# Low halves of a split made by GpSimd instead of VectorE, in the weight conversion and batch 0 of a pack-attention and softplus feed-forward kernel

## Chip, cores and metric

One core of one Trainium2 chip runs the whole program. The time is microseconds on the device for one execution. A core has five engines that run side by side, each through its own instructions in order: TensorE (PE in the profile, its weight loads PEld), VectorE (DVE), ScalarE (ACT), GpSimd (POOL) and SyncE (SP), which here issues nearly all transfers.

## What is computed

For each of 8 batches, 8 heads, 576 rows of 64: 32 packed queries attend to all rows, the rows then attend to the 32 packed results, and the heads are joined to x of 4608 x 512. A feed-forward layer follows.

```python
p_packed = sm_attn(p, k, v)
out = sm_attn(q, p_packed, p_packed)
x = out.transpose(0, 2, 1, 3).reshape(B * S, H * D)
h = x @ w_in                                        # 512 x 2048
g = np.maximum(h, 0.0) + np.log1p(np.exp(-np.abs(h)))   # softplus
return (g @ w_out).astype(np.float32)               # 2048 x 512
```

w_in and w_out come as 64-bit floats; the kernel converts them to 32 bits itself.

## The kernel before

**Units.** The feed-forward part is a loop over 128 units: batch b (8) by slice f of 128 hidden columns (16). A unit has a first product (gemm1, L600), softplus (L622 to L631), and a second product (gemm2_tile, L638), which runs two units later (LAG = 2) and adds to four accumulators acc. The packed results are folded into w_in (make_m, L563), for two slices at a time in batch 0, so that a unit's first product multiplies attention weights with m.

**Split products.** TensorE multiplies in a reduced 32-bit format (F32R), so each factor is split in a high part, the value cast to that format, and a low part, the value less the high part, and a product is three: high by high, high by low, low by high. The halves are at_h and at_l (attention weights, L545 and L546), mh and ml (L578, L579), wo_h and wo_l (w_out, L238 and L244), gh and gl (softplus' result, L614 and L615).

**Softplus of a unit.** ScalarE takes the absolute value of both halves of the product ph (L622), then exp and log (L624, L625; in batch 0 over 576 columns at once). VectorE adds max(h, 0) (L627), which also sets ph free for the next unit, as there are two buffers. Of the 576 rows, GpSimd copies the last 64 into rest (L631). `split` makes gh and gl of the other 512. e has two buffers, gh and gl three each.

**Weight conversion.** `convert` goes through 32 blocks n, 16 of w_in and 16 of w_out. For each, SyncE loads the 64-bit block; ScalarE makes m (L200) and r (L204) from its words; VectorE makes t (a bit mask, L206, and a shift with an or, L211); GpSimd adds t and r as integers (L219), into w_in_sb for a block of w_in and into r for one of w_out. For w_out ScalarE then casts t to wo_h (L238), and wo_l is r less wo_h. m has one buffer and r two for most blocks, so a block's r can be overwritten only when wo_l of an earlier block has been made. Conversion begins before batch 0's attention and goes on through batch 0, beside batch 1's attention.

**What sets the order.** TensorE runs in the order of the code. On the other engines a scheduler orders the instructions from priorities and its own estimate of durations, so a change of engine moves others too. Each engine runs its queue strictly in order.

Of the kernel before, what the change touches and what calls it, by code (L numbers as in the profile page):

```python
# [9 lines left out]
F32 = mybir.dt.float32  # L10
F32R = mybir.dt.float32r
AF = mybir.ActivationFunctionType
ALU = mybir.AluOpType
# [13 lines left out]
def pack_attention_then_softplus_ffn(  # L27
# [10 lines left out]
    nc = tc.nc  # L38
# [3 lines left out]
    P = 128  # L42
# [7 lines left out]
    NT = S // P  # L50
# [26 lines left out]
    def rest_at(b, f):  # L77

        return f + NF if f < LAG and b // 2 % 2 else f
# [69 lines left out]
    def load64(srcs, nm, place):  # L149
        if place is None:  # L150
            x = cv.tile([P, CN], I64, tag="x", name=f"x_{nm}", bufs=2)
        else:
            x = rest[:, place:place + 8, :].rearrange("x f j -> x (f j)").bitcast(I64)
        n = P // len(srcs)
        for i, src in enumerate(srcs):
            nc.sync.dma_start(
                x[i * n:(i + 1) * n].rearrange("x (a n) -> x a n", a=src.shape[1]), src
            )
        return x
# [13 lines left out]
    def convert(order):  # L173

        srcs = {"i": w_in_src, "o": w_out_src}

        places, until = [None, None, LAG, LAG + 8], [len(order), len(order), 6, 16]  # L180
        xs, ts, rs, at = {}, {}, {}, {}

        def prefetch(place):
            n = len(at)
            if n < len(order):
                w, i = order[n]
                at[n] = place
                xs[n] = load64(srcs[w](i), f"{w}{i}", places[place])

        def first(n):  # L190
            x = xs.pop(n)
            lo = x.bitcast(U32).rearrange("x (n two) -> x n two", two=2)[:, :, 0]
            hi = x.bitcast(I32).rearrange("x (n two) -> x n two", two=2)[:, :, 1]
            pool, tm, tr, tt = (work, "gh", "gl", "gh") if spare and n % 2 else (cv, "m", "r", "t")

            m = pool.tile([P, CN], F32, tag=tm, name=f"m_{n}", bufs=LAG + 1 if pool is work else 1)
            nc.scalar.activation(m, hi.bitcast(F32), AF.Copy, scale=2.0**-112)  # L200


            r = pool.tile([P, CN], I32, tag=tr, name=f"r_{n}", bufs=LAG + 1 if pool is work else 2)
            nc.scalar.activation(r, lo, AF.Copy, scale=2.0**-29)  # L204
            t = pool.tile([P, CN], I32, tag=tt, name=f"t_{n}", bufs=LAG + 1 if pool is work else 2)
            nc.vector.tensor_scalar(t, m.bitcast(I32), -0x80000000, None, op0=ALU.bitwise_and)  # L206
            ts[n], rs[n] = (t, m), r

        def second(n):
            t, m = ts[n]  # L210
            nc.vector.scalar_tensor_tensor(  # L211
                t, m.bitcast(I32), 3, t, op0=ALU.logical_shift_left, op1=ALU.bitwise_or
            )
            w, i = order[n]
            dst, a = rs[n], 1
            if w == "i":
                dst, a = w_in_sb.bitcast(I32)[:, :, i * P:(i + 1) * P], DM // P
            v = [y.rearrange("x (a n) -> x a n", a=a) for y in (t, rs[n])]
            nc.gpsimd.tensor_tensor(  # L219
                dst if a > 1 else dst.rearrange("x (a n) -> x a n", a=a), *v, op=ALU.add  # L220
            )

        for n in range(2):
            prefetch(n)
        yield
        for n in range(2, 4):
            prefetch(n)
        yield
        for n in range(len(order) + 1):
            if n < len(order):  # L230
                first(n)
                if n < until[at[n]]:
                    prefetch(at[n])
            yield
            w, i = order[n - 1] if n else ("i", 0)
            t = ts.pop(n - 1)[0].bitcast(F32) if n else None
            if w == "o":
                nc.scalar.copy(wo_h[:, i, :], t)  # L238
            yield
            if n < len(order):  # L240
                second(n)
            yield
            if w == "o":
                nc.vector.tensor_tensor(  # L244
                    wo_l[:, i, :], rs[n - 1].bitcast(F32), wo_h[:, i, :].bitcast(F32),
                    op=ALU.subtract,
                )
                yield
# [358 lines left out]
    def halves(nm):  # L607
        return [
            work.tile([P, NT * P], F32R, tag=t, name=f"{t}_{nm}", bufs=LAG + 1)
            for t in ("gh", "gl")  # L610
        ]

    def split(hi, lo, x):
        nc.vector.tensor_copy(hi, x)  # L614
        nc.vector.tensor_tensor(lo, x, hi.bitcast(F32), op=ALU.subtract)  # L615

    def softplus(b, f, hv, done):
        e = work.tile([P, S], F32, tag="e", name=f"e_{b}_{f}")
        es = [e[:, c * C:(c + 1) * C] for c in range(2)]
        spans = [e] if b == 0 else es  # L620
        for c in range(2):
            nc.scalar.activation(es[c], hv[c], AF.Abs)  # L622
            for x in spans[c:c + 1] if b else spans[:c]:
                nc.scalar.activation(x, x, AF.Exp, scale=-1.0)  # L624
                nc.scalar.activation(x, x, AF.Ln, bias=1.0)  # L625
        for c in range(2):
            nc.vector.scalar_tensor_tensor(es[c], hv[c], 0.0, es[c], op0=ALU.max, op1=ALU.add)  # L627
        yield
        yield
        r = (b % 2) * REST  # L630
        nc.gpsimd.tensor_copy(rest[:, rest_at(b, f), r:r + REST], e[:, NT * P:])  # L631
        yield
        done[b, f] = halves(f"{b}_{f}")
        split(*done[b, f], e[:, :NT * P])

    def gemm2_tile(acc, gh, gl, f, cs, first, last):
        for i, (x, y) in enumerate(((gh, wo_h), (gh, wo_l), (gl, wo_h))):
# [28 lines left out]
    def rests(b):  # L666


        fs = sorted(range(NF), key=lambda x: rest_at(b, x))
        gh, gl = halves(f"{b}_m")  # L670
        n = NT // 2
        for i in range(0, NF, n):
            o = rest_at(b, fs[i])
            c = i % NT * P
            cs = slice(c, c + n * P)
            split(gh[:, cs], gl[:, cs], rest[:, o:o + n, :].rearrange("x f j -> x (f j)"))
            if i == 0:
                yield
                am = ps_acc.tile([P, DM], F32, tag="acc", name=f"acc_{b}_m")
            for t in range(n):  # L680
                gemm2_tile(
                    am, gh, gl, fs[i + t], slice(c + t * P, c + (t + 1) * P),
                    i + t == 0, i + t == NF - 1,
                )
        store(am, [(0, b - 1, NT * P, REST), (REST, b, NT * P, REST)], f"{b}_m", NT)
        yield
# [14 lines left out]

    pt = load_pack(0, (nc.sync, nc.scalar))
    conv = convert(order)
    for g in range(G):
        load("k", 0, g)
# [31 lines left out]
    for u in range(len(units) + LAG):  # L737
        if u < len(units):
            b, f = units[u]
            if f == 0:  # L740
                if (b + 1) % BG == 0 and b + 1 < B:
                    pack_transposed((b + 1) // BG, pt)
                ahead = attention(b + 1) if b + 1 < B else iter(())
                due = 0.0
            chain = softplus(b, f, gemm1(b, f, res[b]), gs)
            next(chain)
            if f == NF - 1:
                if (b + 2) % BG == 0 and b + 2 < B:
                    pt = load_pack((b + 2) // BG, (nc.sync,))
                for _ in ahead:  # L750
                    pass
                if b + 1 < B:
                    weights(b + 1)
# [64 lines left out]
```

## Time and profile before

| | before |
|---|---|
| median of 3 runs | 772.86 us (772.16 to 773.06) |
| the profiled execution | 772.16 us, span 770.4 us |
| TensorE busy | 730.1 us (95%), mean clock 0.98 |
| VectorE, ScalarE, GpSimd busy | 530.7, 433.4, 98.7 us |
| L244 (wo_l) on VectorE | 16, mean 899 ns, all in the first 160 us |
| L615 (gl) on VectorE | 128 over the span, mean 684 ns |
| L219 on GpSimd | 32 in the first 160 us, 44.9 us |

A row of the timeline gives start, length (us), engine, line, operation, output<-inputs with partitions x elements, and in brackets how long the engine had been idle and what released it. A row of the windows gives a stretch, its length, and busy time and count of each engine (of one line, when asked for one), then the granted TensorE clock, the share of the transfer engines and GB/s. The time of an instruction includes what it waits inside the engine once it has begun, so that one kind can show several lengths. A row of the waits gives who waited, for whom, total, times and longest. The chain of waits goes back from the last instruction by what released each.

### The profile page before, as it was taken

To read this page: it belongs to the slowest core of one execution; us is meant where nothing else is said; L and a number is where in the kernel's file an instruction comes from. 1 tells how busy PE (TensorE), PEld (TensorE's weight loads), DVE (VectorE), ACT (ScalarE), POOL (GpSimd) and SP (SyncE) were. 2 spreads that over 40 slices of the span, in tenths; PEclk is the share of its full clock that TensorE was granted. 3 is DMA by queue.
4 is the path that set the end of the run, shared out by engine and by line. 5 is a ranking of instruction groups with operands and counts; after the bars stand their busy time and mean duration, and the time that the engine had idled before them with its cause. 6 is when DMAs were issued, how large, how long until landed. Compare 5 with 4: busy or idle time off the path is not lost.

```text
span 770.4 us, 14175 instructions
## 1 busy us (share of the span) xinstructions
PE 730.1 (95%) x5360; PEld 579.0 (75%) x5360; DVE 530.7 (69%) x1092; ACT 433.4 (56%) x1057; POOL 98.7 (13%) x166
## 2 busy tenths in 40 slices
PE   6557998999999999999999999999999999999997
PEld 4335776787787877887788877877887877888886
DVE  2696879975787568675877568675877558665554
ACT  5667977665555455565455355565555364555540
POOL 1143444200000000000000000000000000000110
PEclk9957999999999999999999999999999999999999
DMA  9877755534312144033312134033312210010002
GB/s 210 231 192 171 180 149 134 123 73 74 65 31 71 30 64 92 1 94 62 68 26 70 31 63 93 1 86 62 63 32 60 40 31 1 1 55 1 1 1 69
DMA packets 149668, 55.97 MB, mean 73 GB/s; under 512 B 116320, under 2 KB 142944, under 8 KB 149600
## 3 DMA queue, kind: packets, MB, share of 16 engines
q1 hardware_dynamic: 149328, 55.00, 32.1%
q8 instruction: 42, 0.69, 0.4%
q14 instruction: 26, 0.21, 0.1%
q10 hardware_dynamic: 272, 0.07, 0.0%
HBM read 45.61 MB, written 9.44 MB: 71 GB/s over the span
## 4 chain that ended last, share of the span: by engine, by line
PE 83%; DVE 6%; ACT 5%; DMA 4%; issue 1%; POOL 1%; SPq 0%; ACTq 0%; DVEq 0%; POOLq 0%
PE acc L638 41%; PE ph L600 26%; PE acc_m L638 6%; PE psm L563 4%; PE ps L277 3%; DMA rest<-in_moe_w_out 2%; DVE at_l L546 1%; PE ps L320 1%; PE psa L312 1%; DMA x_i<-in_moe_w_in 1%; ACT e L624 1%; DVE e L627 1%; ACT m L200 1%; ACT e L622 1%; DVE t L206 1%
## 5 line engine op out<-in xcount | busy, mean ns | idle before, releaser
L638 PE MATMUL acc<-wo_h,gh 128*128 128x512 f32 x512 | 207.7, 406 | 0.0
L627 DVE SCALAR_TENSOR_TENSOR e<-ph,e 128x288 f32<-128x288 f32 x256 | 114.1, 454 | 133.4 <-ACT e L625 130.7
L622 ACT ACTIVATE e<-ph 128x288 f32<-128x288 f32 x256 | 103.0, 403 | 179.5 <-PE ph L600 155.0
L638 PE MATMUL acc<-wo_l,gh 128*128 128x512 f32 x512 | 201.4, 393 | 0.0
L638 PE MATMUL acc<-wo_h,gl 128*128 128x512 f32 x512 | 201.1, 393 | 0.0
L600 PE MATMUL ph<-at_h,mh 128*128 128x288 f32 x512 | 158.5, 309 | 13.1 <-ACT at_h L545 7.2
L600 PE MATMUL ph<-at_l,mh 128*128 128x288 f32 x512 | 153.4, 300 | 3.7 <-DVE at_l L546 3.7
L600 PE MATMUL ph<-at_h,ml 128*128 128x288 f32 x512 | 152.8, 299 | 0.0
L600 PEld LDWEIGHTS ph<-at_h,mh 128*128 128x128 f32 x512 | 97.7, 191 | 48.0 <-DVE gl L615 15.1
L631 POOL COPY rest<-e 128x64 f32<-128x64 f32 x128 | 53.3, 417 | 575.7 <-DVE e L627 542.9
L638 PEld LDWEIGHTS acc<-wo_h,gh 128*128 128x128 f32 x512 | 96.4, 188 | 26.9 <-issue 12.3
L638 PEld LDWEIGHTS acc<-wo_h,gl 128*128 128x128 f32 x512 | 96.3, 188 | 21.2
L624 ACT ACTIVATE e<-e 128x288 f32<-128x288 f32 (+1 forms) x240 | 109.4, 456 | 3.9
L625 ACT ACTIVATE e<-e 128x288 f32<-128x288 f32 (+1 forms) x240 | 109.3, 456 | 3.0
L638 PEld LDWEIGHTS acc<-wo_l,gh 128*128 128x128 f32 x512 | 96.6, 189 | 13.1
L600 PEld LDWEIGHTS ph<-at_l,mh 128*128 128x128 f32 x512 | 97.9, 191 | 8.4 <-DVE at_l L546 5.3
L600 PEld LDWEIGHTS ph<-at_h,ml 128*128 128x128 f32 x512 | 97.9, 191 | 0.0
L615 DVE TENSOR_TENSOR gl<-e,gh 128x512 fp32r<-128x512 f32 x128 | 87.6, 684 | 6.3
L578 ACT CAST mh<-psm 128x512 fp32r<-128x512 f32 (+1 forms) x72 | 36.3, 540 | 60.8 <-PE psm L563 60.6
L614 DVE CAST gh<-e 128x512 fp32r<-128x512 f32 x128 | 55.5, 434 | 5.9
L579 DVE TENSOR_TENSOR ml<-psm,mh 128x512 fp32r<-128x512 f32 (+1 forms) x72 | 43.0, 624 | 22.0 <-ACT mh L578 21.8
L563 PE MATMUL psm<-w_in_sb,pt 64*32 64x512 f32 (+1 forms) x576 | 40.9, 560 | 8.2 <-ACT T_k L269 4.8
(84 smaller groups left out, 694.8 us busy)
## 6 DMA issues: line engine op xcount, KB each, us to landing
v<-in_v SPq DMA_DIRECT2D x16, 576.0 KB, 5.4
x_i<-in_moe_w_in SPq DMA_DIRECT2D x28, 256.0 KB, 4.5
k<-in_k SPq DMA_DIRECT2D x48, 144.0 KB, 3.3
q<-in_q SPq DMA_DIRECT2D x48, 144.0 KB, 3.4
x_o<-in_moe_w_out SPq DMA_DIRECT2D x11, 512.0 KB, 3.7
out<-o SPq DMA_DIRECT2D x18, 256.0 KB, 2.5
rest<-in_moe_w_out SPq DMA_DIRECT2D x5, 512.0 KB, 6.2
k<-in_k SPq DMA_DIRECT2D x4, 576.0 KB, 6.1
```

Source lines behind the costliest of these rows:

```text
L563: nc.tensor.matmul(ps[hh * J:(hh + 1) * J, :n], res["pt"][g][o:o + D, hh * J:(hh + 1) * J], w_in_sb[o:o + D, hh, c * n:(c + 1) * n], start ...
L578: nc.scalar.copy(mh[:, cols], ps[:, :n])
L579: nc.vector.tensor_tensor(ml[:, cols], ps[:, :n], mh[:, cols].bitcast(F32), op=ALU.subtract)
L600: nc.tensor.matmul(ph[:, :C], x[:, ms], y[:, g, cs], start=(i == 0), stop=(i == 3 * G - 1),)
L614: nc.vector.tensor_copy(hi, x)
L615: nc.vector.tensor_tensor(lo, x, hi.bitcast(F32), op=ALU.subtract)
L622: nc.scalar.activation(es[c], hv[c], AF.Abs)
L624: nc.scalar.activation(x, x, AF.Exp, scale=-1.0)
L625: nc.scalar.activation(x, x, AF.Ln, bias=1.0)
L627: nc.vector.scalar_tensor_tensor(es[c], hv[c], 0.0, es[c], op0=ALU.max, op1=ALU.add)
L631: nc.gpsimd.tensor_copy(rest[:, rest_at(b, f), r:r + REST], e[:, NT * P:])
L638: nc.tensor.matmul(acc, x[:, cs], y[:, f, :], start=(first and i == 0), stop=(last and i == 2),)
```

## The change

wo_l of all 16 w_out blocks and gl of batch 0's 16 units go from VectorE to GpSimd. The other batches' gl stays on VectorE, and so does every gh.

```diff
             if w == "o":
-                nc.vector.tensor_tensor(
+                nc.gpsimd.tensor_tensor(
                     wo_l[:, i, :], rs[n - 1].bitcast(F32), wo_h[:, i, :].bitcast(F32),
                     op=ALU.subtract,
                 )
...
-    def split(hi, lo, x):
+    def split(hi, lo, x, engine=None):
         nc.vector.tensor_copy(hi, x)
-        nc.vector.tensor_tensor(lo, x, hi.bitcast(F32), op=ALU.subtract)
+        (engine or nc.vector).tensor_tensor(lo, x, hi.bitcast(F32), op=ALU.subtract)
...
-        split(*done[b, f], e[:, :NT * P])
+        split(*done[b, f], e[:, :NT * P], None if b else nc.gpsimd)
```

TensorE's order is the same in both. VectorE has 32 instructions less, GpSimd 32 more. In the rows below a number behind a name tells tiles of one name apart; e_0 and gl_0 are of unit 0; t_334, r_332 and t_363, r_361 belong to the w_out blocks of slices 2 and 3, t_460, r_458, m_456 and t_561, r_559, m_557 to the next two w_in blocks, and r_581, m_579 to the w_out block behind these.

ScalarE, at the first unit of batch 0, before:

```order
L622 ACTIVATE e_0_541<-ph_0_1_534 128x288 [waits PE_49]
L624 ACTIVATE e_0_541<-e_0_541 128x576 [waits Activation_49]
L238 CAST wo_h<-t_334 128x512 [waits DVE_49]
L200 ACTIVATE m_456<-x_i_246 128x512
L238 CAST wo_h<-t_363 128x512 [waits DVE_49]
L625 ACTIVATE e_0_541<-e_0_541 128x576 [waits Activation_49]
L269 COPY T_k_0_0_555<-psT_k_0_0_551 128x288 [waits PE_49]
```

And with the change:

```order
L238 CAST wo_h<-t_363 128x512 [waits DVE_49]
L622 ACTIVATE e_0_541<-ph_0_1_534 128x288 [waits PE_49]
L204 ACTIVATE r_559<-x_i_288 128x512 [waits DMAHW7_49,DMAHW6_49,Pool_49]
L624 ACTIVATE e_0_541<-e_0_541 128x576 [waits Activation_49]
L200 ACTIVATE m_557<-x_i_288 128x512 [waits DVE_49]
L625 ACTIVATE e_0_541<-e_0_541 128x576 [waits Activation_49]
L204 ACTIVATE r_581<-rest 128x512 [waits DMAHW0_49,Pool_49]
L200 ACTIVATE m_579<-rest 128x512 [waits DVE_49,Activation_49]
L269 COPY T_k_0_0_555<-psT_k_0_0_551 128x288 [waits PE_49]
```

The conversions of two blocks moved ahead of unit 0's exp and log, and r_559, which waits for GpSimd, stands ahead of both.

GpSimd, at the same place, with the change:

```order
L219 TENSOR_TENSOR r_332<-t_334,r_332 128x512 [waits DVE_49,Activation_49]
L219 TENSOR_TENSOR r_361<-t_363,r_361 128x512 [waits DVE_49,Activation_49]
L244 TENSOR_TENSOR wo_l<-r_332,wo_h 128x512 [waits Activation_49,Pool_49]
L244 TENSOR_TENSOR wo_l<-r_361,wo_h 128x512 [waits Activation_49,Pool_49]
L219 TENSOR_TENSOR w_in_sb<-t_460,r_458 128x4x128 [waits DVE_49]
L219 TENSOR_TENSOR w_in_sb<-t_561,r_559 128x4x128 [waits DVE_49,Activation_49]
L631 COPY rest<-e_0_541 128x64 [waits DVE_49,Activation_49]
L615 TENSOR_TENSOR gl_0_570<-e_0_541,gh_0_569 128x512 [waits DVE_49]
```

The two wo_l stand behind both adds and ahead of the two w_in blocks; before, the queue had only the adds and the copy.

GpSimd, in the middle of batch 0 (units 8 and 9), as the difference:

```order
 L219 TENSOR_TENSOR r_1163<-t_1165,r_1163 128x512
+L244 TENSOR_TENSOR wo_l<-r_1163,wo_h 128x512
 L219 TENSOR_TENSOR r_1189<-t_1191,r_1189 128x512
+L244 TENSOR_TENSOR wo_l<-r_1189,wo_h 128x512
 L631 COPY rest<-e_8_1211 128x64
+L615 TENSOR_TENSOR gl_8_1277<-e_8_1211,gh_8_1276 128x512
 L219 TENSOR_TENSOR w_in_sb<-t_1265,r_1263 128x4x128
 L631 COPY rest<-e_9_1320 128x64
+L615 TENSOR_TENSOR gl_9_1363<-e_9_1320,gh_9_1362 128x512
```

Four subtracts of 128x512 join three adds and two small copies there.

## The prediction

> **What bounds the kernel now.** I read the page first: its busy shares and the slices, for the stretch in which TensorE is not full.
>
> ```profile
> PE 730.1 (95%) x5360; PEld 579.0 (75%) x5360; DVE 530.7 (69%) x1092; ACT 433.4 (56%) x1057; POOL 98.7 (13%) x166
> PE   6557998999999999999999999999999999999997
> DVE  2696879975787568675877568675877558665554
> POOL 1143444200000000000000000000000000000110
> PEclk9957999999999999999999999999999999999999
> ```
>
> A slice is 19 us. TensorE is short of full only in the first eight, and just there VectorE and GpSimd are busiest: this is where the weights are converted and batch 0 runs. Behind it TensorE is the bound and the change does nothing. Next I read the windows of the stretch and who made TensorE wait from 60 to 165 us.
>
> ```profile
> 45.00:70.00 25.00, 17.45 (x107) 12.63 (x105) 19.39 (x33) 16.39 (x34) 11.08 (x10) 0.57 0.71 177
> 70.00:136.00 66.00, 60.32 (x513) 45.00 (x511) 56.61 (x119) 55.30 (x117) 30.56 (x28) 1.00 0.63 165
> 136.00:158.00 22.00, 21.74 (x148) 17.41 (x133) 20.44 (x40) 15.29 (x32) 4.80 (x6) 1.00 0.46 89
> PE ph L600 <- DVE e L627: 5.9, 5, 2.8
> PE psm L563 <- POOL w_in_sb L219: 1.7, 1, 1.7
> ```
>
> The columns are window, length, then PE, PEld, DVE, ACT, POOL busy, clock, DMA. From 70 to 136 us TensorE is busy 60.3 of 66 us, VectorE 56.6, ScalarE 55.3, GpSimd 30.6. TensorE's waits after 60 us add up to about 7.6 us, and end in VectorE's softplus row and GpSimd's weight row. By busy shares alone GpSimd has room and VectorE has none, so the shift looks good. What the shares do not tell is whether the two can work at the same time. The timeline of both tells it:
>
> ```profile
> 14.18 1.26 POOL L219 TENSOR_TENSOR w_in_sb<-t,r 128x512 int32<-128x512 int32 x1 [12.88 <-ACT r L204]
> 39.59 0.75 DVE L374 TENSOR_TENSOR a<-a,z 128x576 f32<-128x576 f32 x1
> 39.82 1.65 POOL L219 TENSOR_TENSOR w_in_sb<-t,r 128x512 int32<-128x512 int32 x1 [6.67 <-DVE t L211]
> 40.26 1.82 DVE L546 TENSOR_TENSOR at_l<-aT,at_h 128x576 fp32r<-128x576 f32 x1
> ```
>
> Alone, GpSimd's add takes 1.26 us (14.18). At 39.82 it meets VectorE's L374, which reads two SBUF tiles, and takes 0.39 us more: it runs only when L374 is through at 40.2. VectorE's next two-input subtract, at_l, was ready at 40.26 and ended at 42.08, 0.61 us after GpSimd's end at 41.47, about what it needs alone. So each waits for the other's whole instruction. Other VectorE rows give how long they hold what the two share:
>
> ```profile
> 82.39 0.41 DVE L206 TENSOR_SCALAR t<-m 128x512 int32<-128x512 int32 x1
> 82.72 0.45 DVE L614 CAST gh<-e 128x512 fp32r<-128x512 f32 x1
> 83.09 0.68 DVE L211 SCALAR_TENSOR_TENSOR t<-m,t 128x512 int32<-128x512 int32 x1
> 83.70 0.68 DVE L615 TENSOR_TENSOR gl<-e,gh 128x512 fp32r<-128x512 f32 x1
> 84.30 0.74 DVE L292 TENSOR_REDUCE m<-a 128x1 f32<-128x576 f32 x1
> 67.59 0.24 POOL L631 COPY rest<-e 128x64 f32<-128x64 f32 x1 [4.46 <-ACT a L288]
> ```
>
> From start to start: L206 0.33, L614 0.37, L211 0.61, L615 0.60 us. The bit-mask L206 and the cast L614 are held up by GpSimd too: L206 at 45.21, quoted further down, takes 1.49 us against 0.41 here.
>
> **The change, part by part.** *Off VectorE.* 16 wo_l and 16 gl subtracts, 32 x 0.60 = 19 us of VectorE's own work. Taken alone it could give back at most TensorE's waits on VectorE, the 5.9 us above.
>
> *Onto GpSimd.* 32 floating subtracts with two inputs, 128x512. The trace has none on GpSimd. Bounds from rows: 0.60 us (the same subtract on VectorE) and 1.92 us (eight times GpSimd's 64-column copy at 0.24). I take 1.27, from GpSimd's own two-input add of the same shape at 14.18. Below nothing is excluded, as the instruction occupies GpSimd.
>
> [...]
>
> *The shared port from 70 to 136 us.* The counts are from the windows by line, in the order L206, L211, L614, L615, L244 (VectorE), L219, L631 (GpSimd):
>
> ```profile
> 70.00:136.00 66.00, 10.52 (x19) 1.00 0.63 165
> 70.00:136.00 66.00, 12.31 (x18) 1.00 0.63 165
> 70.00:136.00 66.00, 4.08 (x10) 1.00 0.63 165
> 70.00:136.00 66.00, 6.09 (x9) 1.00 0.63 165
> 70.00:136.00 66.00, 6.42 (x8) 1.00 0.63 165
> 70.00:136.00 66.00, 25.39 (x18) 1.00 0.63 165
> 70.00:136.00 66.00, 5.27 (x10) 1.00 0.63 165
> ```
>
> Held times before, with 18 whole conversions: L206 18 x 0.33 = 5.9, L211 18 x 0.61 = 11.0, L614 10 x 0.37 = 3.7, two softmax steps like that at 39.59 1.3, L219 18 x 1.27 = 22.9, L631 10 x 0.24 = 2.4; with L615 9 x 0.60 = 5.4 and L244 8 x 0.60 = 4.8 that is 57.4 of 66 us, 87%. After: the last two (10.2) go, 17 x 1.27 = 21.6 come, 68.8 us: 104% of the window. So the same work no longer fits. If the port were never free, the stretch grows by 2.8 us; if it is used as densely as now (87%), 79.1 us are needed, 13.1 more. Each side waits for the other's products (gl for gh, L219 for L211), which keeps it from being full; but now it would be the bound, so denser than now. I take the middle, +8. With a subtract of 1.92 us the port needs 79.9 us, +14 to +26; with 0.60 it stays at 57.4 and the term is 0.
>
> *The start of batch 0.* In the new order ScalarE runs L204 r_559 ahead of exp and log of unit 0 (L624, L625). r_559 takes the buffer of r_332, free once wo_l of r_332 has read it, and that is now GpSimd's, behind both L219 adds. Rows of before:
>
> ```profile
> 45.21 1.49 DVE L206 TENSOR_SCALAR t<-m 128x512 int32<-128x512 int32 x1
> 47.17 0.68 ACT L624 ACTIVATE e<-e 128x576 f32<-128x576 f32 x1
> 47.45 2.81 POOL L219 TENSOR_TENSOR r<-t,r 128x512 int32<-128x512 int32 x2 [1.03 <-DVE t L211]
> 49.07 1.74 DVE L244 TENSOR_TENSOR wo_l<-r,wo_h 128x512 fp32r<-128x512 f32 x1 [1.17 <-POOL r L219]
> 49.34 0.68 ACT L625 ACTIVATE e<-e 128x576 f32<-128x576 f32 x1
> 51.79 0.45 DVE L627 SCALAR_TENSOR_TENSOR e<-ph,e 128x288 f32<-128x288 f32 x1
> 53.09 0.38 ACT L269 COPY T_k<-psT_k 128x288 f32<-128x288 f32 x1
> 53.52 1.08 PE L563 MATMUL psm<-w_in_sb,pt 64*32 64x256 f32 x8 [1.99 <-ACT T_k L269]
> ```
>
> GpSimd ends the adds at 50.26, wo_l at 51.53. Then ScalarE's r_559, L624, m_557, L625, at about 0.57 us each (47.17 + 0.68 less the overlap that the rows show): 53.8, and L627 starts there, 2.0 later than 51.79. Queued behind are r_581, m_579 and two T_k copies; the second ends about 55.6, not 53.47, and TensorE's psm and the first product of unit 1 wait for it: +2.1. VectorE no longer stands in wo_l at 49.07, but nothing then waits for that. Upstream of it a subtract of GpSimd can meet at_l or the softmax steps, or miss them: -1.3 to +1.3. I take +2.5, range 0 to 4.
>
> *Others, at nothing.* From 136 on, two conversions, the last wo_l and four gl, some 11 us of GpSimd, lie within the 22 us beside TensorE's 21.7. SP's queue issues two weight loads one place earlier, ahead of k loads that only the attention of the next batch needs. rest copies stand ahead of gl on GpSimd as before. ScalarE's L622 of unit f+2 now waits for gl of f (two e buffers): two units of slack, so it costs only when the port is behind, which is in the term.
>
> **Sum.** The profiled execution took 772.16 us, 1.8 beyond its span of 770.4 and 0.7 under the median of 772.86. 772.16 + 8 + 2.5 = 782.7; against the median 783.4. I say 783.
>
> **Rivals.** *Faster: VectorE was the bound.* VectorE is 56.6 of 66 us busy, and loses a fifth. If a GpSimd subtract holds the port for less than about 1.1 us of the pair's time (17 x 1.1 = 18.7, total 65.9: the window is just full), TensorE's 5.9 and 1.7 us of waits mostly go, say 5 of them: 767. Against it: every meeting in the trace is paid in full. *The same: slack hides it.* The port's surplus of 2.8 us is eaten by waits that TensorE has there anyway, and the start comes out even: 772. Against it: the port would have to be used without a gap. *Much slower: the clock.* TensorE's clock falls after a long gap:
>
> ```profile
> 39.32 0.61 PE L600 MATMUL ph<-at_h,mh 128*128 128x288 f32 x1 [6.69 <-ACT at_h L545]
> 36.00:40.00 4.00, 0.61 (x1) 0.29 (x1) 4.00 (x11) 2.69 (x5) 0.18 (x1) 0.50 0.99 235
> 74.00:78.00 4.00, 2.18 (x15) 1.62 (x13) 2.70 (x6) 3.85 (x8) 2.79 (x3) 1.00 1.12 228
> 61.49 3.25 PE ph L600 x12
> 77.03 1.86 PE ph L600 x12
> ```
>
> After 6.69 us without a product it is at 0.50 and 12 products take 3.25 us (chain of waits); at 1.00 they take 1.86. A gap of some 2 us (74 to 78) leaves it at 1.00. Should the new waits bunch into gaps between these lengths, a unit's 12 first products cost 1.4 us more, and its 12 second ones, 512 columns wide instead of 288, by width 2.5 more; three such units on top of 783 make 795. A slow subtract (1.92 us) ends there too: 772.2 + 2.5 + 20 = 795.
>
> [...]
>
> **Chances and range.** Port saturates, some 774 to 790: 0.64. Clock or slow subtract, 790 and more: 0.15. Same: 0.07. Faster: 0.14. So slower by over 0.2% (1.5 us, about what a measurement of this kernel can tell) 0.79, same 0.07, faster 0.14. The range leaves out the faster case and the worst of the slow one: 772 to 795.
>
> **What would show it.** Right: L615 and L244 on POOL at 1.27 to 1.9 us; L206 and L614 far above 0.45 on the mean in batch 0; POOL near 70% busy from 70 to 140; L624 of unit 0 held until POOL's wo_l is through; TensorE's waits on L627 and w_in up by some 10 us, and everything from batch 1 on moved back by as much. Wrong: POOL subtracts that overlap VectorE's at no cost, or TensorE's waits below 7.6 us.

## The result, and the profile after

The changed kernel takes 782.2 us (median of 4 runs, 781.42 to 783.8), against 772.68 us for the kernel before on the same chip (4 runs). The ratio is 1.0135, 95% interval 1.012 to 1.015: 9.5 us slower. The forecast was 783 us, and "slower" with a chance of 0.79. The profiled execution took 781.42 us, with a span of 779.6.

The page of the kernel after, its busy shares and TensorE's slices:

```profile
PE 728.7 (93%) x5360; PEld 579.7 (74%) x5360; DVE 526.9 (68%) x1060; ACT 434.2 (56%) x1057; POOL 139.3 (18%) x198
PE   5547998899999999999999999999999999999997
```

TensorE's slices 1, 3 and 8 are thinner than before; behind the eighth it is as full as it was. VectorE has lost 32 subtracts: 14.3 us of L244 and 10.9 us of L615 (16 at 0.68) in the trace before. Yet its busy time fell from 530.7 to 526.9 us, by 3.8. The groups of the first 170 us by line, GpSimd's two and three of VectorE's, show where some 15 of the other 21 us went:

```profile
L244 POOL TENSOR_TENSOR wo_l<-r,wo_h 128x512 fp32r<-128x512 f32 x16 | 23.1, 1448 | 0.9
L615 POOL TENSOR_TENSOR gl<-e,gh 128x512 fp32r<-128x512 f32 x16 | 22.8, 1424 | 3.9 <-DVE gh L614 3.6
L211 DVE SCALAR_TENSOR_TENSOR t<-m,t 128x512 int32<-128x512 int32 x32 | 31.3, 981 | 0.5
L206 DVE TENSOR_SCALAR t<-m 128x512 int32<-128x512 int32 x32 | 21.1, 663 | 17.8 <-ACT m L200 17.4
L614 DVE CAST gh<-e 128x512 fp32r<-128x512 f32 x17 | 10.4, 613 | 0.3
```

Behind the bar stand busy time and the mean of one in ns. In the kernel before the same VectorE groups were:

```profile
L211 DVE SCALAR_TENSOR_TENSOR t<-m,t 128x512 int32<-128x512 int32 x32 | 21.7, 682 | 0.4
L206 DVE TENSOR_SCALAR t<-m 128x512 int32<-128x512 int32 x32 | 17.9, 562 | 16.6 <-ACT m L200 16.5
L614 DVE CAST gh<-e 128x512 fp32r<-128x512 f32 x19 | 8.9, 469 | 0.1
```

All three got longer, L211 by 0.30 us, L206 by 0.10 and L614 by 0.14 on the mean, together 15 us: most of what VectorE no longer computes, it now waits inside its instructions. (The rest is in smaller groups and in the overlap of neighbouring rows.) The windows of the steady stretch and the one behind it, after:

```profile
70.00:136.00 66.00, 58.41 (x475) 44.25 (x473) 51.40 (x93) 51.97 (x111) 47.83 (x42) 0.95 0.56 148
136.00:158.00 22.00, 18.43 (x137) 13.89 (x138) 19.29 (x33) 14.06 (x28) 15.15 (x14) 1.00 0.56 125
```

TensorE is busy 58.4 us where it was 60.3, at a mean clock of 0.95 where it was 1.00; GpSimd is busy 72% of the stretch. TensorE's own waits from 60 to 175 us, after:

```profile
PE ph L600 <- DVE e L627: 8.3, 4, 3.2
PE psm L563 <- ACT T_q L269: 2.1, 2, 1.9
PE psm L563 <- ACT a1T L313: 1.3, 1, 1.3
PE psp L320 <- ACT a1T L313: 1.3, 1, 1.3
```

The wait on GpSimd's w_in_sb (1.7 us before) is gone; that on VectorE's L627 rose from 5.9 to 8.3, and 4.7 us on ScalarE's T_q and a1T stand where there were 0.7.

**Where the 9.5 us arose.** The timeline of TensorE tells when each unit's first product begins. Four of these rows, before and after, for unit 1 and for unit 14 of batch 0:

```profile
54.52 0.61 PE L600 MATMUL ph<-at_h,mh 128*128 128x288 f32 x1
141.15 0.40 PE L600 MATMUL ph<-at_h,mh 128*128 128x288 f32 x1 [0.21 <-DVE e L627]
...
57.18 0.61 PE L600 MATMUL ph<-at_h,mh 128*128 128x288 f32 x1
150.49 0.40 PE L600 MATMUL ph<-at_h,mh 128*128 128x288 f32 x1 [3.24 <-DVE e L627]
```

| unit of batch 0 | 0 | 1 | 3 | 4 | 7 | 11 | 13 | 14 | 15 |
|---|---|---|---|---|---|---|---|---|---|
| begins, before (us) | 39.3 | 54.5 | 70.0 | 77.0 | 96.9 | 122.4 | 136.3 | 141.2 | 146.7 |
| later, after (us) | 0.1 | 2.7 | 1.6 | 1.2 | 4.8 | 6.0 | 6.3 | 9.3 | 9.3 |

All of the loss has arisen by unit 15. From unit 0's first product to unit 1's it is 15.2 us before and 17.7 after; from unit 1's to unit 15's, 92.2 and 98.9. So 2.5 us are lost at the start and 6.7 behind it, where the forecast had 2.5 and 8. But the parts lie elsewhere than the forecast put them. Of the start's loss more than half is made up again by unit 4. In the forecast's own stretch, from 70 to 136 us, 4.7 us are added. Another 3.1 us come behind 136 us, where the forecast put nothing, nearly all in one wait of 3.24 us for VectorE's L627.

Behind the start lies something that the forecast gave to a rival. TensorE's clock (third column from the end) is granted at 0.50 in some stretches; its work is slower there (in the prediction's rows 12 products take 3.25 us at 0.50 and 1.86 at 1.00). These are all such stretches from unit 1's first product to unit 15's, the first row before, the others after:

```profile
54.52:66.57 12.05, 9.29 (x53) 7.84 (x49) 8.25 (x15) 8.14 (x16) 4.78 (x4) 0.50 0.95 212
...
57.18:60.16 2.98, 2.98 (x16) 2.98 (x13) 2.49 (x4) 2.16 (x5) 2.90 (x3) 0.50 1.13 209
63.58:66.99 3.41, 3.17 (x13) 3.17 (x14) 0.97 (x3) 0.41 (x1) 2.37 (x3) 0.50 0.47 131
101.12:104.54 3.42, 3.42 (x20) 2.83 (x13) 2.88 (x5) 1.83 (x4) 2.95 (x2) 0.50 0.71 229
128.43:131.84 3.41, 3.41 (x20) 3.36 (x14) 3.41 (x7) 2.27 (x6) 2.72 (x3) 0.50 0.09 20
```

The last two are dips that the kernel before does not have: its clock stays at 1.00 from 66.57 us on. Each follows a thin stretch of TensorE (busy 1.12 of the 2 us from 100, 0.19 of the 2 us from 126). Half of TensorE's busy time at 0.50 is taken here as the most that a stretch can take from it, an estimate from those 12 products, which lose 1.39 of their 3.25 us, 43%: 1.7 us for each dip, 3.4 together. Before 70 us it is the other way round, 4.6 us before and 3.1 after. So by this reckoning the clock accounts for 6.5 - 4.6 = 1.9 of the 6.7 us. TensorE's idle time from unit 1's to unit 15's first product rose by 5.2 us, from 8.7 to 13.9. (The two add up to 7.1, a little more than 6.7; the half is an estimate from above.)

### The profile page after: what moved, and what is told of

It is laid out like the page before. It is cut to its first block, busy times and chain, and to the rows that moved or that the text cites. A ratio compares the mean times of both kernels' runs of the same rounds, so it can differ in the third digit from the quotient of the medians.

```text
span 779.6 us, 14205 instructions
## 1 busy us (share of the span) xinstructions
PE 728.7 (93%) x5360; PEld 579.7 (74%) x5360; DVE 526.9 (68%) x1060; ACT 434.2 (56%) x1057; POOL 139.3 (18%) x198
## 4 chain that ended last, share of the span: by engine, by line
PE 80%; DVE 8%; ACT 5%; DMA 3%; issue 2%; POOL 2%; SPq 0%; DVEq 0%; ACTq 0%; POOLq 0%
PE acc L638 40%; PE ph L600 25%; PE acc_m L638 6%; PE psm L563 4%; PE ps L277 2%; DMA w_in_sb<-in_q 2%; DVE t L211 2%; DVE t L206 1%; PE psa L312 1%; PE ps L320 1%; ACT e L624 1%; DVE e L627 1%; DVE at_l L546 1%; ACT e L622 1%; ACT e L625 1%
## 5 line engine op out<-in xcount | busy, mean ns | idle before, releaser
L627 DVE SCALAR_TENSOR_TENSOR e<-ph,e 128x288 f32<-128x288 f32 x256 | 114.0, 454 | 144.4 <-ACT e L625 141.0
L631 POOL COPY rest<-e 128x64 f32<-128x64 f32 x128 | 51.2, 400 | 562.1 <-DVE e L627 531.8
L600 PEld LDWEIGHTS ph<-at_h,mh 128*128 128x128 f32 x512 | 98.7, 193 | 50.9 <-DVE gl L615 13.4
L624 ACT ACTIVATE e<-e 128x288 f32<-128x288 f32 (+1 forms) x240 | 109.4, 456 | 3.8
L600 PEld LDWEIGHTS ph<-at_h,ml 128*128 128x128 f32 x512 | 98.9, 193 | 0.0
L615 DVE TENSOR_TENSOR gl<-e,gh 128x512 fp32r<-128x512 f32 x112 | 76.7, 685 | 6.6 <-DVE gh L614 0.5
L614 DVE CAST gh<-e 128x512 fp32r<-128x512 f32 x128 | 57.9, 452 | 6.2
L563 PE MATMUL psm<-w_in_sb,pt 64*32 64x512 f32 (+1 forms) x576 | 39.6, 562 | 11.2 <-ACT T_k L269 6.8
```

What stands on the lines that cost most here:

```text
L563: nc.tensor.matmul(ps[hh * J:(hh + 1) * J, :n], res["pt"][g][o:o + D, hh * J:(hh + 1) * J], w_in_sb[o:o + D, hh, c * n:(c + 1) * n], start ...
L600: nc.tensor.matmul(ph[:, :C], x[:, ms], y[:, g, cs], start=(i == 0), stop=(i == 3 * G - 1),)
L615: (engine or nc.vector).tensor_tensor(lo, x, hi.bitcast(F32), op=ALU.subtract)
```

## The experiments

Times are medians; the ratio is to the kernel before, run beside it on the same chip (there 771.5 to 772.0 us). The table holds what the profiled executions gave: from unit 0's first product to unit 1's, from there to unit 15's, the dips of TensorE's clock between 70 us and unit 15, half of TensorE's busy time at a clock of 0.50 from unit 1's to unit 15's first product, dips included, and the time from unit 1 to 15 less that half. The last two columns are worked out and take the slow clock at its full price; part of it may lie in time in which TensorE would have waited anyway.

| kernel | ratio | unit 0 to 1 | unit 1 to 15 | dips | slow clock | less slow clock |
|---|---|---|---|---|---|---|
| before | 1 | 15.2 | 92.2 | 0 | 4.6 | 87.5 |
| after | 1.0135 | 17.7 | 98.9 | 2 | 6.5 | 92.4 |
| wo_l alone | 1.0112 | 17.7 | 96.9 | 1 | 6.1 | 90.7 |
| gl alone | 1.0096 | 15.2 | 99.9 | 2 | 7.5 | 92.4 |
| no low parts | 0.996 | 15.9 | 90.3 | 1 | 5.2 | 85.2 |
| GpSimd writes only | 1.0031 | 17.4 | 93.1 | 0 | 4.7 | 88.4 |
| gl of units 13 to 15 | 0.9995 | 15.2 | 91.8 | 0 | 3.6 | 88.2 |
| staged sum, with the change | 1.0132 | 17.4 | 100.8 | 3 | 8.2 | 92.6 |
| staged sum, without it | 0.9981 | 15.2 | 90.8 | 0 | 3.4 | 87.4 |
| wo_l from slice 6 | 1.013 | 15.2 | 101.3 | 3 | 9.8 | 91.5 |

### What the two engines cost each other

A kernel of its own: VectorE and GpSimd each do eight (beside memsets, 16) instructions of one kind on tiles of 128x512, first alone, then both at once. It writes zeros and computes nothing of the reference.

```diff
+    def d_sub(i):
+        nc.vector.tensor_tensor(dv[i % 2], a, b, op=ALU.subtract)
...
+    def g_sub(i):
+        nc.gpsimd.tensor_tensor(gp[i % 2], a, b, op=ALU.subtract)
...
+        (d_sub, 8, g_sub, 8), (d_cast, 8, g_sub, 8), (d_max, 8, g_sub, 8), (d_psum, 8, g_sub, 8),
+        (d_sub, 8, g_copy, 8), (d_sub, 16, g_set, 16), (d_cast, 16, g_set, 16),
```

The last two lines are the stages with both engines: how many of what VectorE does, and how many of what GpSimd does (a cast, a reduce and a subtract from PSUM on VectorE; a one-input copy and a memset on GpSimd).

> Measures the disputed cost by itself; it computes nothing of the reference and writes zeros. Stages of 8 or 16 instructions of 128x512 on VectorE alone, GpSimd alone, and both at once on data of their own. Port theory: GpSimd's subtract takes about 1.27 us alone and VectorE's 0.60; both at once, eight pairs take 8 x (0.60 + 1.27) = 15 us, the cast beside it 8 x (0.35 + 1.27) = 13 us, and the reduction and the subtract with one operand in PSUM run at their own pace, 8 x 1.27 = 10.2 us in all. Rival, the queue: the engines do not hold each other up, GpSimd is only slow, and every paired stage takes 10.2 us. A GpSimd instruction that only writes should hold up neither, or only the cast.

Its timeline, VectorE's and GpSimd's rows, first alone, then together:

```profile
4.06 4.89 DVE L65 TENSOR_TENSOR dv<-a,b 128x512 fp32r<-128x512 f32 x8
9.20 2.78 DVE L69 CAST dv<-a 128x512 fp32r<-128x512 f32 x8 [0.26 <-ACT a L55]
23.11 9.80 POOL L81 TENSOR_TENSOR gp<-a,b 128x512 fp32r<-128x512 f32 x8 [22.67 <-ACT b L56]
52.37 12.36 DVE L65 TENSOR_TENSOR dv<-a,b 128x512 fp32r<-128x512 f32 x8 [29.71 <-ACT b L56]
52.41 13.43 POOL L81 TENSOR_TENSOR gp<-a,b 128x512 fp32r<-128x512 f32 x8 [0.40 <-ACT b L56]
66.75 10.23 DVE L69 CAST dv<-a 128x512 fp32r<-128x512 f32 x8 [2.02 <-ACT a L55]
66.95 11.15 POOL L81 TENSOR_TENSOR gp<-a,b 128x512 fp32r<-128x512 f32 x8 [1.11 <-ACT h L59]
78.75 9.81 POOL L81 TENSOR_TENSOR gp<-a,b 128x512 fp32r<-128x512 f32 x8 [0.64 <-ACT ai L57]
109.19 9.72 DVE L65 TENSOR_TENSOR dv<-a,b 128x512 fp32r<-128x512 f32 x16 [0.82 <-ACT b L56]
119.63 8.70 DVE L69 CAST dv<-a 128x512 fp32r<-128x512 f32 x16 [0.72 <-ACT a L55]
```

GpSimd's subtract takes 1.22 us (9.80 / 8). Two subtracts side by side take 13.4 us for eight pairs, near the sum of the two (14.7) and far from the longer (9.8). Beside a reduce (78.75) GpSimd loses nothing: 9.81 us for eight, 9.80 alone. So exclusion is real here, and depends on the kind. But a VectorE subtract costs its partner (13.43 - 9.80) / 8 = 0.45 us and a cast (11.15 - 9.80) / 8 = 0.17, not the 0.61 and 0.35 that they last. Either way some 0.17 us of each pair overlap; the runs do not tell whose 0.17 us these are. VectorE is the one that pays: its eight subtracts go from 4.9 to 12.4 us, its casts from 2.8 to 10.2. Beside GpSimd's memset, which only writes, the subtract keeps its 0.61 us (9.72 / 16); the cast, at 0.54 (8.70 / 16) against 0.35 alone, does not. "The shared port" is the forecast's name for this exclusion; the runs show who waits and how long, and not what lies behind it.

### Each half of the change alone

wo_l alone, against the changed kernel:

```diff
-        split(*done[b, f], e[:, :NT * P], None if b else nc.gpsimd)
+        split(*done[b, f], e[:, :NT * P])
```

gl alone, against the changed kernel (the subtract is L244):

```diff
-                nc.gpsimd.tensor_tensor(
+                nc.vector.tensor_tensor(
```

> Only wo_l goes to GpSimd; gl of batch 0 stays on VectorE. Port theory: from 70 to 136 us the shared port is wanted 57.4 + 8 x 0.67 = 62.8 of 66 us (95%), some +3 us, and the start's +2.5 us (r waits for wo_l on GpSimd) stays: 778, 775 to 781. Rival, the queue: what costs is that ScalarE's r waits for wo_l behind other GpSimd work, so nearly the whole 9.5 us is here: 782.

> Only batch 0's gl goes to GpSimd; wo_l stays on VectorE. Port theory: 57.4 + 9 x 0.67 = 63.4 of 66 us (96%), some +3 us, nothing at the start: 776, 773 to 779. Rival, the queue: gl has two units of slack, so its lateness costs nothing: 772.7.

Measured: wo_l alone 780.06 us, 1.0112 (1.0097 to 1.0127); gl alone 778.6 us, 1.0096 (1.0079 to 1.0113). Alone they lose 8.1 and 6.6 us, together 9.5: they do not add up. The start's loss comes with wo_l (17.7 us against 15.2). Behind it, with the slow clock taken out, wo_l alone loses 3.2 us, gl alone 4.9, and both together 4.9.

### VectorE relieved, with nothing for GpSimd

wo_l and batch 0's gl are not made at all; TensorE multiplies the high parts in their place, as often as before. Two places of the edit, against the kernel before:

```diff
-                nc.vector.tensor_tensor(
-                    wo_l[:, i, :], rs[n - 1].bitcast(F32), wo_h[:, i, :].bitcast(F32),
-                    op=ALU.subtract,
-                )
...
-        for i, (x, y) in enumerate(((gh, wo_h), (gh, wo_l), (gl, wo_h))):
+        for i, (x, y) in enumerate(((gh, wo_h), (gh, wo_h), (gl, wo_h))):
```

> Leaves out wo_l (all) and gl of batch 0 altogether; TensorE multiplies as often, with the high parts in their place. It prices what relief of VectorE is worth with no GpSimd work in exchange. Port theory: the port is wanted 47.2 of 66 us (72%), TensorE's 7.6 us of waits on VectorE and on the weights after 60 us go in part: 768, 765 to 771. Rival, the scheduler's new order: the order that comes with low parts taken off VectorE is itself at fault, then this is not faster than 772.7.

Measured: 768.98 us, 0.996 (0.9944 to 0.9976), 3.0 us faster. Its window of the steady stretch:

```profile
70.00:136.00 66.00, 62.52 (x519) 47.19 (x518) 46.97 (x100) 56.13 (x118) 26.28 (x28) 0.97 0.65 161
```

VectorE falls from 56.6 to 47.0 us, and TensorE only gains 2.2. This is about what the change could have brought with GpSimd for nothing: 3 us, for 25 us of work taken off VectorE. (ScalarE's order is here that of the changed kernel, row for row, and the start takes 15.9 us, not 15.2.) Its busy share was no measure of what it held up.

### GpSimd as busy, but hardly reading

GpSimd subtracts 16 columns and then writes the rest twice with memsets, so most of the low parts are left out. VectorE's and ScalarE's order is that of the changed kernel, row for row.

```diff
+    def low(dst, x, hi, n=16):
+        nc.gpsimd.tensor_tensor(dst[:, :n], x[:, :n], hi[:, :n], op=ALU.subtract)
+        for i in range(2):
+            nc.gpsimd.memset(dst[:, n - 4:].bitcast(F32), 0.0)
```

> The changed kernel, but GpSimd subtracts only the first 16 columns of each low part and fills the other 496 with zeros in two memsets, so the low parts are left out; it is busy about as long (0.15 + 2 x 0.5 us), what waits for it waits as long, and the order on VectorE and ScalarE is that of the changed kernel row for row. In the measurement of the cost by itself such a memset left VectorE's two-input subtract at 0.61 us. Port theory: VectorE's L211 falls from 0.98 to about 0.75 us, and most of the loss goes: 775, 773 to 777. Rival, the queue: nothing changes, 781 to 783. Rival, the order: nothing changes either, 781 to 783.

Measured: 774.44 us, 1.0031 (1.0022 to 1.004). In this kernel L216 is the shift with an or (L211 elsewhere) and L211 the mask (L206 elsewhere); groups of the first 170 us, and the steady window:

```profile
L211 DVE TENSOR_SCALAR t<-m 128x512 int32<-128x512 int32 x32 | 24.8, 776 | 20.6 <-ACT m L205 17.4 <-POOL wo_l L176 1.3 <-POOL wo_l L174 0.9
L216 DVE SCALAR_TENSOR_TENSOR t<-m,t 128x512 int32<-128x512 int32 x32 | 21.8, 685 | 0.5
70.00:136.00 66.00, 60.13 (x513) 45.05 (x513) 49.31 (x99) 56.37 (x118) 50.58 (x82) 1.00 0.65 167
```

GpSimd is as busy as in the changed kernel (50.6 us against 47.8), in the same order, and 2.7 us of loss remain of the 9.5. L211's kind is back at 685 ns, the clock at 1.00, and unit 1 to 15 at 93.1 us. With the slow clock taken out it is 88.4, against 92.4 in the changed kernel and 87.5 before. So it is mainly not GpSimd's being busy, nor the new order, but its reading two tiles that costs the steady part. The mask is longer here (776 ns) than in the changed kernel (663), at hardly any loss; that of the two the shift with an or is the one that hurts is argued from this and not tested alone, as other two-input instructions are relieved here too. What stands behind it is told by ScalarE's waits from 70 to 150 us, before, after and here:

```profile
ACT wo_h L238 <- DVE t L211: 0.3, 1, 0.3
...
ACT wo_h L238 <- DVE t L211: 4.4, 5, 1.5
...
ACT wo_h L243 <- DVE t L216: 0.5, 2, 0.3
```

ScalarE's cast wo_h waits for a stretched L211, and in ScalarE's queue the next unit's exp and log stand behind it. gl alone has no such wait and still loses; there wo_l on VectorE stretches (1015 ns a piece against 899), and from 70 to 150 us ScalarE's r waits 2.8 us for GpSimd's w_in_sb and 2.2 us for its gl, where before it waited 1.6 us in all. So with gl alone GpSimd's being occupied may cost as well, and how much of that loss is the reading was not tested. The start's loss stays here too (17.4 us). The kernel without low parts has the same order on ScalarE and 15.9, so it comes in the main from GpSimd's being occupied.

### gl where the port is free

Only gl of batch 0's last three units goes to GpSimd; wo_l is VectorE's. The line of the changed kernel, and here:

```diff
-        split(*done[b, f], e[:, :NT * P], None if b else nc.gpsimd)
+        split(*done[b, f], e[:, :NT * P], nc.gpsimd if (b, f) > (0, 12) and b == 0 else None)
```

> The kernel before with only the gl of units 13, 14 and 15 of batch 0 on GpSimd, when the conversion is nearly done and VectorE is at its fullest (20.4 of 22 us from 136 to 158). Port theory: few weight instructions are left to meet, so no loss: 772 within 1.5 us, perhaps 1 us gained. Rival, the queue: gl on GpSimd costs by its length wherever it stands, 3 of 16 of the 6.6 us of gl alone, 773.2; if the late units are where gl alone lost its 5 us, 775 or more.

Measured: 771.55 us, 0.9995 (0.9985 to 1.0006). The three subtracts take 1.43 us each on GpSimd, no less than in the changed kernel, and cost nothing where weights are no longer converted beside them.

### The cause of the start's loss: three tries

The forecast held that r_559 waits for wo_l of r_332. The trace after shows just that wait, in the rows of ScalarE:

```profile
50.89 0.67 ACT L204 ACTIVATE r<-x_i 128x512 int32<-128x512 uint32 x1 [1.76 <-POOL wo_l L244]
51.47 0.67 ACT L624 ACTIVATE e<-e 128x576 f32<-128x576 f32 x1
55.44 0.68 ACT L269 COPY T_k<-psT_k 128x288 f32<-128x288 f32 x2
```

To take it away, the integer sum of a w_out block was put into a free stretch of w_in_sb, so that r is free at once; once with the change and once without.

```diff
+            if w == "o" and 2 <= i < NF - 2:
+                dst = sums[n] = w_in_sb.bitcast(I32)[:, :, (NF - 2 + i % 2) * P:(NF - 1 + i % 2) * P]
+                a = DM // P
...
+                    (sums[n - 1] if n - 1 in sums else rs[n - 1]).bitcast(F32),
```

> The changed kernel, but the sum of t and r of a w_out block (slices 2 to 13) goes to columns of w_in_sb that are converted last, and wo_l reads it there, so ScalarE's next r no longer waits for wo_l on GpSimd. Port theory: the start's loss goes, 2.7 us at unit 1, the rest stays: 779.5, 778 to 781. Rival, the queue (ScalarE held by r): 773 to 775.

> The same edit of the kernel before, where wo_l is VectorE's. Both theories: r was free early enough there, 772 within 1.5 us; if ScalarE's r did wait for a late wo_l now and then, some 2 us less, 770.

These two tell nothing on the question: 784.82 us, 1.0168 (1.0151 to 1.0185), and 779.57 us, 1.0096 (1.0078 to 1.0114). The columns chosen still held batch 0's q, which the sum partly overwrote, and TensorE's transposes of q waited 17.0 and 15.5 us for GpSimd's sum. With columns that are free:

> As the staged sum before, but in columns of w_in_sb that batch 0's q does not use (those of slices 8 and 9 for w_out slices 2 to 7, of 14 and 15 for 8 to 13), so nothing of batch 0's attention can wait for it; VectorE's and ScalarE's order is that of the changed kernel row for row. Port theory with the start as I forecast it (ScalarE's r_559 waits for wo_l on GpSimd): unit 1 begins some 15 us after unit 0 instead of 17.8, and the time is 779.5, 778 to 781. Rival, the order: r_559 stands ahead of exp and log and that is what costs at the start, not what it waits for; then unit 1 still begins 17 us after unit 0 and the time stays at 781 to 783.

> The same edit of the kernel before. Both theories: 772 within 1.5 us; 770 if ScalarE's r waited for wo_l on VectorE now and then. A gain would make it a version that beats both kernels.

With the change: 782.16 us, 1.0132 (1.0098 to 1.0166). Without it: 770.61 us, 0.9981 (0.9968 to 0.9994). ScalarE's rows of the first, where L636 is exp, and L281 is T_k:

```profile
49.57 0.67 ACT L204 ACTIVATE r<-x_i 128x512 int32<-128x512 uint32 x1
50.13 0.68 ACT L636 ACTIVATE e<-e 128x576 f32<-128x576 f32 x1
52.00 0.67 ACT L200 ACTIVATE m<-x_i 128x512 f32<-128x512 f32 x1 [1.19 <-DVE t L211]
54.53 0.67 ACT L204 ACTIVATE r<-rest 128x512 int32<-128x512 uint32 x1 [1.29 <-POOL w_in_sb L223]
55.71 0.68 ACT L281 COPY T_k<-psT_k 128x288 f32<-128x288 f32 x2
```

r_559 no longer waits, and exp comes 1.3 us earlier. But the next, m_557, waits for an L211 that GpSimd's wo_l stretched to 1.64 us, and r_581 waits for GpSimd's w_in_sb, which stands behind the two wo_l. The T_k copies come at 55.71 instead of 55.44, and unit 1 only 0.3 us earlier behind unit 0 (17.4 us). The wait that the forecast named was real, and taking it away gave next to nothing, as the rival had it. But that r_559 stands ahead of exp and log is not what costs either: so it does in the kernel without low parts, where unit 1 comes 15.9 us after unit 0. (The time tells little here, as the four executions spread from 778.96 to 784.92 us.)

One part of the start's loss is order alone, and lies ahead of r_559. TensorE, in unit 0's own product, waits for the second at_l. The rows of TensorE and of VectorE's masks, before and after:

```profile
44.40 0.61 PE L600 MATMUL ph<-at_l,mh 128*128 128x288 f32 x1 [0.26 <-DVE at_l L546]
43.27 0.41 DVE L206 TENSOR_SCALAR t<-m 128x512 int32<-128x512 int32 x1
...
45.93 0.61 PE L600 MATMUL ph<-at_l,mh 128*128 128x288 f32 x1 [1.67 <-DVE at_l L546]
43.39 1.81 DVE L206 TENSOR_SCALAR t<-m 128x512 int32<-128x512 int32 x2
```

Before, VectorE runs wo_l and one mask ahead of this at_l; with the change, an L211 and two masks, of which one meets GpSimd's L219. That makes at_l 1.5 us later (45.13 against 43.60), and TensorE's wait 1.4 us longer. No wo_l runs on GpSimd at that moment. The wait of 1.67 us is the same in the kernels with wo_l alone, without low parts, with GpSimd only writing and with the staged sum, where VectorE has the same two masks ahead of it. In the one without low parts half of these 1.4 us is made up again before unit 1. So of the 2.5 us the new order by itself costs 0.7, and wo_l on GpSimd the other 1.8. Next, wo_l itself was kept off GpSimd for the first six slices:

```diff
-                nc.gpsimd.tensor_tensor(
+                (nc.gpsimd if i > 5 else nc.vector).tensor_tensor(
```

> The change, but the wo_l of the first six of the 16 slices of w_out stays on VectorE; GpSimd makes wo_l of slices 6 to 15 and all of batch 0's gl. If the loss at the start comes from GpSimd's wo_l standing where slices 0 and 1 are prepared (whichever of the waits there ends last), the step from unit 0's first product to unit 1's goes back from 17.8 to about 15.2 us, as in the kernel before, and the time is about 779.6 us (778 to 781): the steady loss stays. Rival: what is saved at the start is given back in the units after it, as with the staged sum, and the time stays at 782.

Measured: 781.67 us, 1.013 (1.011 to 1.0149). Unit 1 comes 15.2 us after unit 0, as before the change. So the loss at the start is GpSimd's wo_l there, by whichever wait ends last, with the order that comes with it: ScalarE's and VectorE's order at the start is here again that of the kernel before. The time is that of the rival. Of the 2.5 us saved, 0.4 are left at unit 4, which begins at 77.03 us before, at 77.82 here and at 78.22 in the changed kernel. Up to there the clock is at 0.50 longer here: from unit 1's first product to 70 us it takes 4.7 us by the reckoning of the table, against 3.1 in the changed kernel. At unit 4 a dip follows, seen in the windows of this kernel, against those of the kernel before around the same gap:

```profile
76.00:78.00 2.00, 0.18 (x2) 0.18 (x2) 1.58 (x4) 2.00 (x6) 0.93 (x1) 1.00 1.12 231
78.00:80.00 2.00, 2.00 (x10) 2.00 (x11) 2.00 (x4) 1.05 (x3) 1.95 (x3) 0.55 1.14 228
...
76.00:78.00 2.00, 0.97 (x7) 0.97 (x8) 1.62 (x5) 1.85 (x4) 1.66 (x2) 1.00 1.13 225
78.00:80.00 2.00, 2.00 (x15) 1.78 (x14) 2.00 (x4) 1.52 (x4) 1.02 (x1) 1.00 1.17 240
```

TensorE waits for L627 there in both, each time in a gap of 1.82 us:

```profile
77.82 0.40 PE L600 MATMUL ph<-at_h,mh 128*128 128x288 f32 x1 [1.82 <-DVE e L627]
...
77.03 0.40 PE L600 MATMUL ph<-at_h,mh 128*128 128x288 f32 x1 [1.82 <-DVE e L627]
```

In the one the clock falls to 0.50, in the other it stays at 1.00; no run shows what decides between the two. Three dips, each of up to 1.7 us by the same estimate, stand in this profile, against two in the changed kernel's. By the table, the slow clock takes 9.8 us of unit 1 to 15 here and 6.5 in the changed kernel; the 3.3 us between them are more than the 2.5 saved at the start, and with the slow clock taken out this kernel is 0.9 us shorter there. How the clock ran in the other executions of these kernels is known only as a mean over the whole, and no experiment here held the dips still. So their share of the time is worked out, not shown.

### A version to beat both?

The kernel before with the staged sum was 0.9981. It was run with the late gl added (the sum that is staged is that of w_out):

> The kernel before with two edits: GpSimd's sum of w_in goes to free columns first (alone: 0.9981 of the kernel before), and gl of units 13 to 15 of batch 0 goes to GpSimd (alone: 0.9995). If both hold and add up, 770.3 us, 0.998 of the kernel before. If the gain of the staged sum was chance, 771.9. If the late gl collides with GpSimd's loads once the units come earlier, above 772.

Measured: 771.2 us, 0.9992 (0.9983 to 1.0). The two small gains did not add up, and the 1.4 us of the staged sum are at the edge of what can be told; in its profile 1.2 of them are the slow clock's (3.4 us against 4.6). No version here is shown to be faster than the kernel before by more than that.

## Why the prediction was right, point by point

**What bounds the kernel.** Right: the loss arises in the first eight slices, and from batch 1 on all is only moved back, by 9.3 us at unit 15.

**Off VectorE.** The forecast allowed up to 5.9 us, and the "faster" rival about 5. Without any low parts the kernel gains 3.0. The faster rival ended at 767; its best case would have been 769.

**Onto GpSimd.** 1.27 us was taken; alone it is 1.22, in the kernel 1.42 to 1.45 with what it waits.

**The shared port, +8.** The kind of cost was right, its size was not. In the term's own stretch, 70 to 136 us, 4.7 us were lost, not 8, and up to 3.4 of them are the price of the two dips, which the term does not have. The step that failed is "each waits for the other's whole instruction": some 0.17 us of each pair overlap. The row it was read from has it: L374 ends at 40.34, and the add that began at 39.82 lost 0.39 of those 0.52 us, not all. With 0.45 us for every two-input instruction and 0.17 for a mask or a cast (an estimate: 0.45 was measured on a subtract and 0.17 on a cast, neither on L211 or L206), the same counts give about 47 of 66 us before and 61 after, 71% and 92%. So by this sum the port was never over-full, the 104% came of overstated prices, and "now it would be the bound" is wrong. The loss comes from meetings in queues that run in order: an L211 that meets a GpSimd subtract ends up to 1.1 us late (the longest L211 takes 1.77 us, and 0.70 before), and what stands behind it comes late too. The kernel in which GpSimd only writes shows that the reading does most of it.

**The start, +2.5.** The size came out (2.5), the cause is half right, and so the size is in part luck. It is wo_l on GpSimd for 1.8 us of it, but not by r_559's wait alone, as the staged sum showed, and hardly by its reading, as the kernel in which GpSimd only writes showed. What comes upstream, at_l and the softmax steps, was taken at about nothing (-1.3 to +1.3): there TensorE lost 1.4 us, by VectorE's new order and not by a subtract of GpSimd, and 0.7 of these are left at unit 1 where GpSimd makes no low parts. The start's term does not simply add to the steady one either: of 2.7 us at unit 1, 1.2 are left at unit 4.

**At nothing.** SyncE's queue, the rest copies and the e buffers left no mark among TensorE's larger waits. The tail after 136 us was not free: 3.1 us are lost between unit 13 and unit 14, where TensorE waits 3.24 us for L627 and had waited 0.21. In the kernel in which GpSimd only writes, with the same order on ScalarE and VectorE, this wait is 1.7 us, so about half of it stays without the reading.

**The sum.** 782.7 was reckoned and 782.2 measured, but the port's term was too large, the tail's was missing and part of the start's loss was made up again; that these errors cancel to within 1 us is luck. What holds is the direction, that GpSimd's reading holds VectorE up, and that r_559 would wait.

**Rivals.** The clock was given 0.15 and as a case of its own, at 795. It came as a part of the likeliest case, two dips at 1.7 us each where 3.9 had been reckoned for a unit: each dip lasts 3.4 us (3.42 and 3.41), not a unit long. As the clock before 70 us is slow for less time than in the kernel before, only 1.9 us net are its part.

**What would show it.** L244 and L615 at 1.45 and 1.42 us (forecast 1.27 to 1.9), L206 and L614 at 0.66 and 0.61 (far above 0.45), GpSimd 72% busy from 70 to 136 us (near 70%), L624 held behind r_559 till GpSimd's wo_l is through: all seen. "TensorE's waits on L627 and w_in up by some 10 us" was wrong: together they rose from 7.6 to 8.3 us, ScalarE's took their place, and some of the loss is not a wait but a slower clock.

## What to carry to other kernels

Before moving work from VectorE to GpSimd, ask what VectorE does at the same moment: a two-input GpSimd instruction held up the masks, casts and two-input instructions there (by 0.10, 0.14 and 0.30 us on the mean of L206, L614 and L211), so that here 25 us taken off VectorE left it only 3.8 us less busy. Bound the gain first by leaving the work out altogether (here 3 us), and count as loss not the sum of held times but what stands behind the stretched instruction in each queue. Compare the start of every unit before and after, not only the total: here the total came out and its parts did not. And where TensorE's clock is at half in some stretches, sum these over the whole part that is compared, in both kernels: counting only the dips behind 70 us would have put 3.4 us down to the clock, where it is 1.9.

## What the runs showed of the hardware that was not expected

- Two exclusive instructions overlap by some 0.17 us, whether VectorE's is a subtract of 0.61 us or a cast of 0.35. VectorE pays more for a meeting than GpSimd does: eight casts went from 2.8 to 10.2 us, eight GpSimd subtracts beside them from 9.8 to 11.2.
- GpSimd's one-input copy is held up too, and holds up: seven take 6.70 us beside VectorE subtracts (each 0.56 alone, 0.96 there), and eight of these subtracts 7.90 us (4.89 alone).
- A reduce, or a subtract that reads one input from PSUM, costs GpSimd's subtract nothing (9.81 and 9.82 us for eight, 9.80 alone).
- TensorE's clock fell after a gap of 1.82 us in one kernel and not in another. The two dips of the changed kernel behind 70 us lasted 3.42 and 3.41 us at a clock of 0.50, which by the estimate above takes up to 1.7 us each.
